# Attention and MLP kernel on one core: loads tied to the first pair, and a new layout of PSUM banks in the first chunk

## The chip, the cores and the metric

One core of a Trainium2 chip. The metric is device time in microseconds (us), the median of several executions. TensorE is called PE below, VectorE DVE, ScalarE ACT, GpSimd POOL, and the queue that issues the loads SP.

## The reference

Two parts, one after the other. The first is a linear attention with a decaying state (batch 4, 8 heads, 768 time steps, head dimension 48):

```
for t in range(S):
    kt, vt, rt = (k[:, :, t], v[:, :, t], r[:, :, t])
    cur = np.einsum('bhd,bhe->bhde', u[None] * kt, vt)
    y[:, :, t] = np.einsum('bhd,bhde->bhe', rt, state + cur)
    state = w[None, :, :, None] * state + np.einsum('bhd,bhe->bhde', kt, vt)
```

The second is an MLP over its 3072 result rows of 384 numbers: `h = x @ w_in` (384 to 2048), exact GELU, then `@ w_out` (2048 to 384). All in float32.

## The kernel before

**Work.** Time is cut into 6 chunks of 128 steps. In a chunk the 8 heads are 4 pairs, and a pair in a chunk is a *group*: 24 groups, numbered by `gi`. A group's operands are `T` (r and k, lanes by time), `N` (k and v, time by lanes). DVE scales `T` by powers of the decay (L357), POOL scales `N` (L363). PE makes `scores` and `own` (L390, keys against queries, into banks `g.x`), `gains` (L401, what the group adds to the state, into columns from `U0` of `g.y`), `old` (L409, the carried state against the queries) and `new` (L419, masked scores against v), both into `g.y`. DVE selects the masked scores into `Am` (L447, `select`). ACT and DVE split the result in `g.y` into a high and a low part (L461, L462, `keep`), which are x of the MLP. ACT or DVE update the state from `gains` (L439, L442, `state`). In the first chunk the 16 rows of padding of a pair's x come from the pair `p = 3`, which is group 0: a matmul `gaps` (L429) brings them from group 0's result `x3`, so the `gaps` of groups 1 to 3 need group 0's `keep`.

**MLP.** 96 *steps* (6 chunks by 16 blocks of 128 hidden units). Step m has nine products into bank `Hp` (L544, `moe1`), GELU twice on ACT (L572, L573), a subtraction on DVE (L574), and nine products into three banks `O` (L585, `moe2`), mostly one step later. Each weight block comes as 64-bit words (`raw`, 768 KB, L301) and in chunk 0 is split into a high and a low float by three ACT and four DVE instructions (L314 to L326, `w_split`). The three `raw` buffers are used in turn.

**Order.** Nothing is ordered by hand. `Plan` collects all operations with a planned length, a due time and the names that they read and write; `run` then puts them into the engines' queues, earliest due first among those whose planned inputs are ready. Semaphores are set by the layer below from the tiles that the instructions really touch; a name given to `Plan` alone orders the queues and makes no semaphore. `GROUP_DUE` says how late in a period of four steps a group is due, `GROUP_AHEAD` how far ahead of that its loads are.

**First chunk.** Groups 0 to 3 (`first_group`) use two sets of PSUM banks in turn (`SETS`): `A` and `Y` for even groups, `AE` and `YE` for odd ones. A bank holding a set's results must be read before the next group of the same set writes it. PE begins with `HEATS` products of zeros, and `plan.filler` may put more of them into planned pauses. Loads are listed by `LOADS`: groups 1 to 5, three weight blocks, and u. Every load also waits for the load eight places ahead of it in the queue, since eight semaphores (`DMAHW0` to `DMAHW7`) are used in turn.

## Time and profile before

| what | value |
|---|---|
| median of 3 executions | 517.97 us (517.8 to 518.02) |
| the profiled execution's own time | 519.95 us |
| its span, first to last instruction | 517.9 us |
| PE, matmuls | 488.1 us, 94% |
| DVE | 245.5 us, 47% |
| ACT | 207.1 us, 40% |
| POOL | 65.7 us, 13% |
| mean granted clock of PE | 0.96 of 2.4 GHz |
| DMA | 43.85 MB, 85 GB/s |

The shares are means over three stages: the first chunk's groups (0 to 41 us), the stage in which weights are still split (to about 135 us), and the rest. A busy PE is not a PE at its peak: matmuls are pipelined, and the granted clock says at which of its two levels (1.2 or 2.4 GHz) it ran.

### The profile page before, as it was taken

The numbers are of one execution on the slowest core, as the hardware profiler recorded it, in microseconds if no ns is written. First come the engines' busy times: TensorE is split into PE (matmuls) and PEld (weight loads), VectorE is DVE, ScalarE is ACT, GpSimd is POOL, SyncE is SP. The second block draws the span as 40 slices with busy tenths as digits, with TensorE's granted clock in tenths as the row PEclk, the third lists the DMA queues.
The fourth block names the chain that finished last, engine by engine and source line by source line (L and its number), as shares of the span: only waits on it lengthen the run. The fifth ranks groups of instructions, "written<-read, shape, count | busy, mean of one in ns | idle before, by whom it ended". The sixth has DMA issues, their size and how long they took to land.

```text
span 517.9 us, 11402 instructions
## 1 busy us (share of the span) xinstructions
PE 488.1 (94%) x5006; PEld 389.5 (75%) x5006; DVE 245.5 (47%) x366; ACT 207.1 (40%) x435; POOL 65.7 (13%) x66
## 2 busy tenths in 40 slices
...
GB/s 224 321 113 63 196 155 221 208 129 92 53 93 92 43 51 92 84 61 94 47 48 92 68 77 92 66 28 92 90 54 92 6 7 10 63 0 1 0 1 65
DMA packets 13190, 43.85 MB, mean 85 GB/s; under 512 B 1808, under 2 KB 2192, under 8 KB 13136
## 3 DMA queue, kind: packets, MB, share of 16 engines
q1 hardware_dynamic: 13136, 43.07, 26.9%
q8 instruction: 41, 0.67, 0.6%
q14 instruction: 13, 0.11, 0.1%
...
## 4 chain that ended last, share of the span: by engine, by line
PE 85%; DVE 6%; issue 3%; DMA 3%; ACT 1%; POOL 1%; SPq 0%; POOLq 0%
PE Hp L544 37%; PE O L585 35%; PE Y L419 3%; PE A L390 3%; PE Y L409 3%; PE Y L401 1%; DMA Nb<-in_rkv_dram 1%; DMA T<-in_rkT_dram 1%; DVE wl L326 1%; PE Y L585 1%; DVE wa L322 1%; DVE Sa L442 1%; PE AE L390 1%; ACT gh L572 1%; DVE gl L574 1%
## 5 line engine op out<-in xcount | busy, mean ns | idle before, releaser
L544 PE MATMUL Hp<-xx,wh 128*128 128x512 f32 x576 | 170.0, 402 | 2.1 <-issue 0.7
L574 DVE TENSOR_TENSOR gl<-gf,gh 128x512 fp32r<-128x512 f32 x95 | 75.9, 799 | 183.4 <-ACT gf L573 183.2
L572 ACT ACTIVATE gh<-Hp 128x512 fp32r<-128x512 f32 x95 | 56.8, 598 | 179.3 <-PE Hp L544 179.1
L544 PEld LDWEIGHTS Hp<-xx,wh 128*128 128x128 f32 x576 | 106.4, 190 | 27.3 <-ACT gf L573 1.8
L544 PE MATMUL Hp<-xx,wl 128*128 128x512 f32 x288 | 84.8, 402 | 1.4 <-DVE wl L326 1.2
L585 PE MATMUL O<-gh,wh 128*128 128x512 f32 (+1 forms) x285 | 81.8, 394 | 2.9 <-ACT gh L572 2.7
L585 PE MATMUL O<-gh,wl 128*128 128x512 f32 (+1 forms) x285 | 80.6, 390 | 0.0
L585 PE MATMUL O<-gl,wh 128*128 128x512 f32 (+1 forms) x285 | 80.6, 390 | 0.0
L585 PEld LDWEIGHTS O<-gh,wh 128*128 128x128 f32 x285 | 52.6, 188 | 19.6 <-ACT gh L572 7.8
L544 PEld LDWEIGHTS Hp<-xx,wl 128*128 128x128 f32 x288 | 54.0, 190 | 17.1 <-DVE wl L326 3.5
L585 PEld LDWEIGHTS O<-gl,wh 128*128 128x128 f32 x285 | 52.6, 188 | 11.8 <-DVE gl L574 0.2
L585 PEld LDWEIGHTS O<-gh,wl 128*128 128x128 f32 x285 | 52.6, 188 | 11.6
L573 ACT ACTIVATE gf<-Hp 128x512 f32<-128x512 f32 x96 | 56.9, 593 | 0.0
L361 POOL TENSOR_TENSOR Nb<-Nb 128x384 f32<-128x384 f32 x16 | 21.0, 1315 | 262.5 <-DMA Nb<-in_rkv_dram 227.2
L381 ACT ACTIVATE Am<-diag,cs 128x64 f32<-128x64 f32 x128 | 33.9, 342 | 27.6 <-DVE cs L376 27.6
L442 DVE SCALAR_TENSOR_TENSOR Sb<-Sa,E,Y 48x192 f32<-48x192 f32 x40 | 16.5, 413 | 35.4 <-ACT xx L461 28.0
L363 POOL TENSOR_TENSOR Nb<-Nb,WN 128x384 f32<-128x384 f32 x20 | 21.5, 1076 | 59.3 <-DMA Nb<-in_rkv_dram 58.1
L461 ACT CAST xx<-Y 112x512 fp32r<-112x512 f32 (+1 forms) x16 | 9.4, 586 | 42.5 <-PE Y L401 38.7
L357 DVE TENSOR_TENSOR Tb<-Tb,E 112x1024 f32<-112x1024 f32 x20 | 24.4, 1219 | 2.3 <-DMA Tb<-in_rkT_dram 2.3
L447 DVE COPY_PREDICATED Am<-past,A 128x512 f32<-128x512 uint32 x22 | 16.2, 736 | 8.9 <-PE A L390 6.0
L373 POOL TENSOR_TENSOR Nb<-Nb,u_sb 128x384 f32<-128x384 f32 x16 | 17.7, 1106 | 0.1
L326 DVE TENSOR_TENSOR wl<-wa,wh 128x768 fp32r<-128x768 f32 x16 | 17.4, 1089 | 0.2
...
## 6 DMA issues: line engine op xcount, KB each, us to landing
...
```

The lines of the kernel that those rows point to most:

```text
L326: add("dve", sdve(n), LATER, lambda: nc.vector.tensor_tensor(out=both(wl), in0=af, in1=both(wh).bitcast(F32), op=ALU.subtract), r=[A_, f"w ...
L357: add("dve", sdve(1024), LATER, lambda: nc.vector.tensor_tensor(out=flat, in0=flat, in1=E[:, 0, g.p].rearrange("l h i -> l (h i)").unsquee ...
L361: add("pool", pool(DM), LATER, lambda: nc.gpsimd.tensor_tensor(out=g.n[:, 0], in0=g.n[:, 0], in1=g.n[:, 1], op=ALU.mult), r=[g.K], w=[g.R])
L363: add("pool", pool(DM), LATER, lambda: nc.gpsimd.tensor_tensor(out=g.kn, in0=g.kn, in1=WN[:, g.p].rearrange("s j d -> s (j d)").unsqueeze( ...
L381: add("act", sact(HALF) + 60, LATER, lambda x=x, b=b: nc.scalar.activation(out=g.am[:, x, b, :], in_=diag2, func=AF.Copy, scale=g.sums[:, ...
L390: nc.tensor.matmul(g.x[times(h), x, col + b * HALF:col + (b + 1) * HALF], lhsT=k_, rhs=g.t[quarter(x), 0, b, times(h)], start=True, stop=True)
L442: add("dve", 420, at, lambda l=l, x=x, more=more: nc.vector.scalar_tensor_tensor(out=g.s[h + 1][quarter(1 - x)], in0=g.s[h][l], scalar=E[l ...
L544: nc.tensor.matmul(O[3], lhsT=wt[j][:, 0, k_ * 128:(k_ + 1) * 128], rhs=x[:, a, k_, :], start=start and k_ == ks[0], stop=stop and k_ == k ...
L572: add("act", 480, LATER, lambda: nc.scalar.activation(out=high, in_=O[3], func=AF.Gelu), r=["H"], w=[GH])
L573: add("act", 480, LATER, lambda: nc.scalar.activation(out=gf, in_=O[3], func=AF.Gelu), r=["H"], w=["gf"])
L574: add("dve", dve(512), LATER, lambda: nc.vector.tensor_tensor(out=low, in0=gf, in1=high.bitcast(F32), op=ALU.subtract), r=["gf", GH], w=[GL])
L585: nc.tensor.matmul(bank(dst)[:, a:b], lhsT=wt[j][:, 1, d * 128:(d + 1) * 128], rhs=gt[:, a:b], start=(j == 0 and n == 0), stop=(j == NJ - ...
```

## The change

The four loads named in `GATED` (weight block 2, groups 4 and 5, u) are given to the planner as readers of `x3h`, the high part of group 0's result, and `w2` goes ahead of group 5 in `LOADS`. Groups 1 to 3 are loaded and planned in the order of their numbers. In the first chunk scores alternate between `AA` and `AE` as before, all four groups share `YU` for `old`, `new` and `gaps`, and `gains` have a tile of their own, `UE`, with a half for even and a half for odd groups. `GROUP_DUE` grows from 9500 to 20000 ns. The hold on the filler is set at the first `gains` and not taken back.

```
-WEIGHT_AHEAD, GROUP_AHEAD, GROUP_DUE = 12500, 28000, 9500
+WEIGHT_AHEAD, GROUP_AHEAD, GROUP_DUE = 12500, 28000, 20000
...
-LOADS = (1, "w0", 2, 3, "w1", 4, 5, "w2", "u")
+LOADS = (1, "w0", 2, 3, "w1", 4, "w2", 5, "u")
+GATED = ("w2", 4, 5, "u")
...
-        AE, YE = (pso.tile([128, 2, 512], F32, name=n) for n in ("AE", "YE"))
+        AE = pso.tile([128, 2, 512], F32, name="AE")
+        UE = pso.tile([128, 2, 512], F32, name="UE")
...
-                (g.x, g.X), (g.y, g.Y) = SETS[i if gi < NP else 0]
+                g.x, g.X = (AE, ["O0", "O1"]) if gi < NP and i else (AA, ["A0", "A1"])
+                g.y, g.Y = YU, ["Y0", "Y1"]
+                g.u, g.U, g.u0 = (UE, ["O2", "H"], i * 256) if gi < NP else (YU, g.Y, U0)
...
-            add("pe", 500, LATER, first_gains, r=[g.K, g.V], w=g.Y)
+            add("pe", 500, LATER, lambda: (setattr(plan, "hold", True), gains(g)), r=[g.K, g.V], w=g.U)
...
+        for gi in range(NP):
+            if gi:
+                load_group(gi, gi + 3)
+            first_group(gi)
...
         for n, x in enumerate(LOADS):
+            early_ = ["x3h"] if x in GATED else []
+            if x in range(NP):
+                continue
...
-                w_load(int(x[1]), n + 3)
+                w_load(int(x[1]), n + 3, early_)
             else:
-                load_group(x, n + 3)
-        for gi in range(NP):
-            first_group(gi)
+                load_group(x, n + 3, early_)
```

How it moves instructions, first on SP: the loads from group 3's (or 2's) first to u. `T_102` to `T_105` and `N_110` to `N_113` are groups 0 to 3, `Tb_106`, `Nb_114` group 4, `Tb_107`, `Nb_115` group 5, `raw_130` weight block 2; in brackets what a load waits for. Before:

```order
L205 DMA T_105<-in_rkT_dram 112x1024
L207 DMA N_113<-in_rkv_dram 128x768
L205 DMA T_104<-in_rkT_dram 112x1024
L207 DMA N_112<-in_rkv_dram 128x768 [waits DMAHW0_49]
L301 DMA raw_128<-in_wmlp_dram 128x1536 [waits DMAHW1_49]
L301 DMA raw_129<-in_wmlp_dram 128x1536 [waits DMAHW2_49]
L205 DMA Tb_106<-in_rkT_dram 112x1024 [waits DMAHW3_49]
L209 DMA Nb_114<-in_rkv_dram 128x768 [waits DMAHW4_49]
L205 DMA Tb_107<-in_rkT_dram 112x1024 [waits DMAHW5_49]
L209 DMA Nb_115<-in_rkv_dram 128x768 [waits DMAHW6_49]
L301 DMA raw_130<-in_wmlp_dram 128x1536 [waits DMAHW7_49]
L696 DMA u_sb<-in_uN_dram 64x384 [waits DMAHW0_49]
```

Now:

```order
L206 DMA T_104<-in_rkT_dram 112x1024
L208 DMA N_112<-in_rkv_dram 128x768
L206 DMA T_105<-in_rkT_dram 112x1024
L208 DMA N_113<-in_rkv_dram 128x768 [waits DMAHW0_49]
L302 DMA raw_128<-in_wmlp_dram 128x1536 [waits DMAHW1_49]
L302 DMA raw_129<-in_wmlp_dram 128x1536 [waits DMAHW2_49]
L206 DMA Tb_106<-in_rkT_dram 112x1024 [waits DMAHW3_49]
L210 DMA Nb_114<-in_rkv_dram 128x768 [waits DMAHW4_49]
L302 DMA raw_130<-in_wmlp_dram 128x1536 [waits DMAHW5_49]
L206 DMA Tb_107<-in_rkT_dram 112x1024 [waits DMAHW6_49]
L210 DMA Nb_115<-in_rkv_dram 128x768 [waits DMAHW7_49]
L700 DMA u_sb<-in_uN_dram 64x384 [waits DMAHW0_49]
```

Groups 2 and 3 have changed places, and weight block 2 has gone ahead of group 5. No load waits for ACT, the engine that writes `x3h`; each waits for one of the eight DMA semaphores alone, as before.

Second on PE: the first chunk, from group 1's `own` to group 1's `new` (a plain matmul of this list is two in the trace, so x16 here is x32 there; the `gaps` are single). Before:

```order
L390 MATMUL AE<-T_103,KB_109 64x64 x16
L401 MATMUL YE<-N_111 48x48 x16
L409 MATMUL Y<-T_102,Sb 48x64 x8
L419 MATMUL Y<-Am_116,N_110 48x64 x16
L390 MATMUL AE<-T_105 64x64 x16
L390 MATMUL AE<-T_105,KB_109 64x64 x16
L390 MATMUL A<-T_104 64x64 x16
L429 MATMUL YE<-x_122,spread 128x256 x4
L409 MATMUL YE<-T_103,Sb 48x64 x8
L419 MATMUL YE<-Am_117,N_111 48x64 x16
```

Now, on to group 3's `own`:

```order
L393 MATMUL AE<-T_103,KB_109 64x64 x16
L412 MATMUL Y<-T_102,Sb 48x64 x8
L422 MATMUL Y<-Am_116,N_110 48x64 x16
L404 MATMUL UE<-N_111 48x48 x16
L393 MATMUL A<-T_104 64x64 x16
L393 MATMUL A<-T_104,KB_108 64x64 x16
L432 MATMUL Y<-x_122,spread 128x256 x4
L412 MATMUL Y<-T_103,Sb 48x64 x8
L422 MATMUL Y<-Am_117,N_111 48x64 x16
L404 MATMUL UE<-N_112 48x48 x16
L393 MATMUL AE<-T_105 64x64 x16
L393 MATMUL AE<-T_105,KB_109 64x64 x16
```

Group 0's `old` and `new` now stand ahead of group 1's `gains`, and one group ends before the next but one begins. Behind this piece come, now, for group 2 `gaps`, `old`, `new`, then group 3's `gains`, `gaps`, `old`, `new`, and the first step of the MLP.

Third on DVE: the first steps of the MLP, around weight block 1 (`wl1_84` is its last piece). Before:

```order
L318 TENSOR_SCALAR wa1_132<-wa1_132 128x768
L357 TENSOR_TENSOR Tb1_107<-Tb1_107,E_98 112x1024
L320 SCALAR_TENSOR_TENSOR wa1_132<-raw1_129,wa1_132 128x768
L447 COPY_PREDICATED Am0_116<-diag2_94,A_67 128x512
L322 ISA wa1_132<-wa1_132,wb1_135 128x1536
L442 SCALAR_TENSOR_TENSOR Sb_97<-Sa_96,E_98,Y_68 48x192 x2
L447 COPY_PREDICATED Am0_116<-past2_95,A_67 128x512
L442 SCALAR_TENSOR_TENSOR Sa_96<-Sb_97,E_98,Y_68 48x192 x2
L326 TENSOR_TENSOR wl1_84<-wa1_132,wh1_76 128x768
L574 TENSOR_TENSOR gl0_125<-gf_127,gh0_123 128x512
```

Now:

```order
L321 SCALAR_TENSOR_TENSOR wa1_132<-raw1_129,wa1_132 128x768
L319 TENSOR_SCALAR wa2_133<-wa2_133 128x768
L323 ISA wa1_132<-wa1_132,wb1_135 128x1536
L569 TENSOR_TENSOR gl0_125<-gf_127,gh0_123 128x512
L321 SCALAR_TENSOR_TENSOR wa2_133<-raw2_130,wa2_133 128x768
L327 TENSOR_TENSOR wl1_84<-wa1_132,wh1_76 128x768
L323 ISA wa2_133<-wa2_133,wb0_134 128x1536
L360 TENSOR_TENSOR Tb1_107<-Tb1_107,E_98 112x1024
L450 COPY_PREDICATED Am0_116<-diag2_94,A_67 128x512
L327 TENSOR_TENSOR wl2_85<-wa2_133,wh2_77 128x768
```

The seven instructions of groups 4 and 5 that stood ahead of `wl1` in the first piece now stand behind it. The same shift by part of a period runs through the rest of the lists. Ahead of step 16 (the second chunk of the MLP), though, both PE lists hold the products of the same groups: `gains` of five and `old` and `new` of four behind the first chunk. Ahead of weight block 15's last DVE instruction the old DVE list has 154 rows and the new one 155: a sum over a group (L376) and a GELU subtraction (L574) more, a state update (L442) less.

## Rows read from the trace of the kernel before

**Rows 1.** Windows: us, busy time (and instructions) of PE, PEld, DVE, ACT, POOL, clock, DMA

```profile
13.00:26.00 13.00, 6.36 (x206) 5.76 (x200) 7.06 (x11) 5.95 (x12) 2.52 (x3) 0.50 1.03 324
39.00:52.00 13.00, 11.15 (x184) 7.88 (x184) 10.91 (x18) 8.53 (x14) 0.00 (x0) 0.70 0.19 63
60.00:135.00 75.00, 69.55 (x697) 51.62 (x696) 69.79 (x96) 48.07 (x75) 9.73 (x7) 1.00 0.45 149
135.00:515.00 380.00, 374.35 (x3416) 302.22 (x3414) 137.18 (x206) 133.08 (x312) 46.83 (x42) 1.00 0.19 57
```

**Rows 2.** Timeline, PE, first chunk: start, duration, engine, line, operation, count, idle before

```profile
18.03 0.45 PE L409 MATMUL Y<-T,Sb 48*48 48x64 f32 x3 [2.76 <-issue]
...
21.14 1.06 PE L390 MATMUL A<-T 48*64 48x64 f32 x27
26.85 0.48 PE L390 MATMUL A<-T 48*64 48x64 f32 x5 [4.65 <-issue]
...
33.74 0.87 PE L401 MATMUL YE<-N 64*48 64x48 f32 x26 [0.32 <-issue]
```

**Rows 3.** The page's table of DMA queues: packets, MB, share of 16 engines

```profile
q8 instruction: 41, 0.67, 0.6%
```

**Rows 4.** Timeline, group 5's operands on POOL and DVE

```profile
28.17 0.99 POOL L363 TENSOR_TENSOR Nb<-Nb,WN 128x384 f32<-128x384 f32 x1 [1.70 <-DMA Nb<-in_rkv_dram]
...
44.16 1.22 DVE L357 TENSOR_TENSOR Tb<-Tb,E 112x1024 f32<-112x1024 f32 x1
```

**Rows 5.** Timeline, PE, ACT and DVE in the first chunk, pieces of one group

```profile
27.26 1.22 PE L429 MATMUL YE<-x,spread 112*128 112x256 f32 x4
28.41 1.09 PE L409 MATMUL YE<-T,Sb 48*48 48x64 f32 x16
29.60 1.10 PE L419 MATMUL YE<-Am,N 64*48 64x64 f32 x32
30.48 1.08 PE L390 MATMUL A<-T,KB 48*64 48x64 f32 x32
31.33 0.86 PE L401 MATMUL Y<-N 64*48 64x48 f32 x32
...
38.90 0.58 ACT L461 CAST xx<-YE 128x512 fp32r<-128x512 f32 x1 [3.56 <-PE YE L419]
...
39.52 0.69 DVE L462 TENSOR_TENSOR xx<-YE,xx 128x512 fp32r<-128x512 f32 x1 [2.14 <-ACT xx L461]
...
39.77 1.11 PE L419 MATMUL Y<-Am,N 64*48 64x64 f32 x32
...
41.21 0.77 PE L544 MATMUL Hp<-xx,wh 128*128 128x512 f32 x1 [0.33 <-DVE Sa L442]
```

**Rows 6.** Timeline, DVE while weights are split, and POOL beside it

```profile
47.51 0.73 DVE L447 COPY_PREDICATED Am<-diag,A 128x512 f32<-128x512 uint32 x1 [1.26 <-PE A L390]
...
60.90 0.55 DVE L318 TENSOR_SCALAR wa<-wa 128x768 int32<-128x768 int32 x1
...
61.37 0.94 DVE L326 TENSOR_TENSOR wl<-wa,wh 128x768 fp32r<-128x768 f32 x1
...
103.53 1.77 DVE L326 TENSOR_TENSOR wl<-wa,wh 128x768 fp32r<-128x768 f32 x1
...
104.56 1.61 POOL L363 TENSOR_TENSOR Nb<-Nb,WN 128x384 f32<-128x384 f32 x1
105.22 1.36 DVE L318 TENSOR_SCALAR wa<-wa 128x768 int32<-128x768 int32 x1
...
106.51 1.75 DVE L326 TENSOR_TENSOR wl<-wa,wh 128x768 fp32r<-128x768 f32 x1
...
128.84 1.52 DVE L326 TENSOR_TENSOR wl<-wa,wh 128x768 fp32r<-128x768 f32 x1
```

**Rows 7.** Chain that ended last: start us, us, what

```profile
42.11 3.78 PE Hp L544 x8
...
156.19 2.10 PE O L585 x9
```

More of the change, by code (lines that the diff above doesn't have):

```diff
@@ L200, in rwkv_gelu_mlp, with load_group @@
         slot = lambda gi: gi if gi < NP else NP + gi % 2
-        def load_group(gi, at):
+        def load_group(gi, at, r=()):
             s = slot(gi)
-            dma(LP * 4096, at, lambda: nc.sync.dma_start(T[s], rkT[gi]), w=[f"T{s}"])
+            dma(LP * 4096, at, lambda: nc.sync.dma_start(T[s], rkT[gi]), r=r, w=[f"T{s}"])
             if gi < NP:
-                dma(C * 3072, at + 1, lambda: nc.sync.dma_start(N[s], rkv[gi, :, 1:]), w=[f"Nk{s}", f"Nv{s}"])
+                dma(C * 3072, at + 1, lambda: nc.sync.dma_start(N[s], rkv[gi, :, 1:]), r=r, w=[f"Nk{s}", f"Nv{s}"])
             elif gi < DIRECT:
-                dma(C * 3072, at + 1, lambda: nc.sync.dma_start(N[s][:, 1:], rkv[gi, :, 1:]), w=[f"Nk{s}", f"Nv{s}"])
+                dma(C * 3072, at + 1, lambda: nc.sync.dma_start(N[s][:, 1:], rkv[gi, :, 1:]), r=r, w=[f"Nk{s}", f"Nv{s}"])
             else:
-                dma(C * 4608, at + 1, lambda: nc.sync.dma_start(N[s], rkv[gi]), w=[f"Nr{s}", f"Nk{s}", f"Nv{s}"])
+                dma(C * 4608, at + 1, lambda: nc.sync.dma_start(N[s], rkv[gi]), r=r, w=[f"Nr{s}", f"Nk{s}", f"Nv{s}"])
         dma(5000, 0, lambda: nc.sync.dma_start(wu_sb, wuT), w=["w_sb"])
@@ L252, in warm_up @@
             for n in range(HEATS):
-                heat((A + [YU[:, 0], YU[:, 1]] + [AE[:, 0], AE[:, 1], YE[:, 0]])[n % 7])
-            plan.filler = lambda: heat(YE[:, 1]), "H", HEAT_NS, HEAT_ROOM
-        add("pe", 430 * HEATS, 10, warm_up, r=["zeros"], w=["H", "A0", "A1", "O0", "O1", "O2", "Y0", "Y1"])
+                heat((A + [YU[:, 0], YU[:, 1]] + [AE[:, 0], AE[:, 1]])[n % 6])
+            plan.filler = lambda: heat(UE[:, 1]), "H", HEAT_NS, HEAT_ROOM
+        add("pe", 430 * HEATS, 10, warm_up, r=["zeros"], w=["H", "A0", "A1", "O0", "O1", "Y0", "Y1"])
         E0, E1 = (E[:, a].rearrange("l p h i -> l (p h) i") for a in range(2))
@@ L298, in rwkv_gelu_mlp, with w_load @@
         wbits = wmlp.bitcast(I32)
-        def w_load(j, at):
+        def w_load(j, at, r=()):
             dma(128 * 6144, at, lambda: nc.sync.dma_start(raw[j % 3].rearrange("p h n t -> p (h n t)"), wbits[:, j]),
-                w=[f"raw{j % 3}"])
+                r=r, w=[f"raw{j % 3}"])
         def w_split(j):
@@ L400, in gains @@
                     for h in range(2 if g.more else 1):
-                        nc.tensor.matmul(g.y[quarter(x), h, U0 + b * D:U0 + (b + 1) * D], lhsT=g.kn[times(h), b, heads(x)],
+                        nc.tensor.matmul(g.u[quarter(x), h, g.u0 + b * D:g.u0 + (b + 1) * D], lhsT=g.kn[times(h), b, heads(x)],
                                          rhs=g.vn[times(h), b, heads(x)], start=True, stop=True)
@@ L436, in state @@
                 l = quarter(x)
-                more = g.y[l, h, U0:U0 + NB * D].rearrange("d (b e) -> d b e", e=D)
+                more = g.u[l, h, g.u0:g.u0 + NB * D].rearrange("d (b e) -> d b e", e=D)
                 if g.c == 0 and h == 0:
                     add("act", 320, at, lambda x=x, more=more: nc.scalar.copy(out=g.s[1][quarter(1 - x)], in_=more),
-                        r=[g.Y[0]], w=[g.S[1][1 - x]])
+                        r=[g.U[0]], w=[g.S[1][1 - x]])
                 else:
@@ L443, in state @@
                         out=g.s[h + 1][quarter(1 - x)], in0=g.s[h][l], scalar=E[l, 1, g.p, h, MID:MID + 1], in1=more,
-                        op0=ALU.mult, op1=ALU.add), r=[g.Y[h], g.S[h][x], "E1"], w=[g.S[h + 1][1 - x]])
+                        op0=ALU.mult, op1=ALU.add), r=[g.U[h], g.S[h][x], "E1"], w=[g.S[h + 1][1 - x]])
         def select(g, mask, MASK, col):
@@ L477, in first_group @@
             add("pe", 600, LATER, lambda: own(g), r=[g.T, f"{g.KB}0", f"{g.KB}1"], w=g.X)
-            def first_gains():
-                gains(g)
-                if gi % 2:
-                    plan.hold = True
-            add("pe", 500, LATER, first_gains, r=[g.K, g.V], w=g.Y)
+            add("pe", 500, LATER, lambda: (setattr(plan, "hold", True), gains(g)), r=[g.K, g.V], w=g.U)
             state(g, 0, LATER)
@@ L492, in first_group @@
             state(g, 1, LATER)
-            if gi % 2:
-                add("do", 0, LATER, lambda: setattr(plan, "hold", False), w=g.Y)
         def products(g, f):
@@ L505, in products @@
                 r += [f.T, f.K, f.V] + ([f"{f.KB}0", f"{f.KB}1"] if f.direct else [])
-                w += f.X + f.Y
+                w += f.X + f.U
                 ns += 1300 if f.direct else 850
```

5 lines of the change are left out of this document (2 added, 3 removed).

## The prediction, made before the changed kernel ran

> **What bounds the kernel now.** I read the windows by stage first. From 135 to 515 us PE is busy for 374.35 of 380 us [rows 1]: there the end moves only by work or idle time of PE itself. From 60 to 135 us PE and DVE are both busy for 93% of the time (69.55 and 69.79 of 75) [rows 1]; 16 weight blocks are split then, and what DVE does later, the MLP does later. In the first chunk it is neither: from 13 to 26 us PE is busy for 6.36 of 13 us, DVE for 7.06, and the DMA engines without a break (share 1.03) [rows 1].
>
> Next the timeline of PE in the first chunk. It stands still three times for nothing that the profile shows: 2.76 us up to 18.03, 4.65 us up to 26.85, and 0.32 us up to 33.74 [rows 2]. Between the first and the second restart lie 126 matmuls (3, three times 32, 27), between the second and the third 127 (5, 4, 16, three times 32, 6). An equal number of instructions each time speaks for the program itself being fetched: the instruction queue moved 41 packets [rows 3] for PE's 10,012 matmuls and weight loads, one per 244. I take it that PE waits for a packet of code, asked for when the packet before is begun, and that it comes late while the data loads fill the DMA engines.
>
> The Trainium skill speaks against this reading (Runtime: NRT & Kernel Launch, Instruction fetch mechanics): the next block is fetched while the current one runs, and crossing into it is "mostly hidden". Here the trace differs with 2.76 and 4.65 us [rows 2], and the sum goes by the trace; by the rule of the Trainium skill these waits would be something else and might stay away, for 511 us instead of 516.7, as the third rival works out from rows.
>
> **The loads.** The change means to hold four loads until group 0's result. In the built queue none waits for ACT; all wait for the same eight DMA semaphores as before. So I cost the holding at nothing, neither gain nor loss. What is left is order. Weight block 2 goes ahead of group 5's two loads, which so come later by 768 KB at 324 GB/s [rows 1], 2.4 us. POOL scales that group at 28.17 now, its T is scaled at 44.16 [rows 4]: some 13 us of cover, without which it would cost those 2.4 us. Groups 2 and 3 swap places with equal sizes: nothing. The zero products stay twelve.
>
> **The first chunk on PE.** I put the new order onto the old restarts. Up to the first stop PE ran 221 matmuls, in the new list 29 of the 32 of group 0's `new` are then through; the second stop falls 8 matmuls into group 1's `new`, the third 4 into group 2's `old`. Up to 26.85 the waits cover all else. From there, with start-to-start times at the same half clock [rows 5]: rest of `new` 0.66 (24 of 32 at 0.88), `gains` 0.86, `scores` and `own` 1.70, `gaps` 1.15, four of `old` 0.2: 31.4. The code that came at 33.74 before [rows 2] comes then again, so PE waits 2.3 instead of 0.32 us. After it: rest of `old` 0.99 (1.19 less 0.2), `new` 0.88, to 35.6. Group 3's `gains` (0.86) hide only part of what follows: all groups now share one tile for results, so group 3's `gaps` wait until group 2's result is read. `new` began at 34.73; 1.17 us after such a beginning ACT reads, 0.62 later DVE starts, 0.69 it takes [rows 5], and 0.1 for the handing over makes 37.3, 0.8 us of idle PE. Then `gaps` 1.15, `old` 1.19, and 1.44 from the beginning of `new` to step 0 (39.77 to 41.21) [rows 5]: 41.1 against 41.21. **Term: -0.1.** Before, PE came to this point late, held by DVE reading the odd set of banks; that wait goes, and the code is late next. If the third packet is there when wanted, step 0 comes 2.3 us sooner; if it needs as long after the second as the second after the first (8.82 us), it lands at 35.67 and step 0 comes 1.8 us later than now. Both ends go into the range.
>
> **The stage of splits.** Ahead of step 16 both PE lists hold the same groups, and DVE's lists to the last weight block are 154 and 155 rows long. The larger `GROUP_DUE` therefore takes no work out of this stage; it changes what stands beside what. Two things follow. First, DVE stood idle for 1.26 us at 47.51, waiting for PE's scores of group 4 [rows 6]; there the new list has pieces of blocks 1 and 2, whose data landed long before. Between nothing and 1.3 us to gain; I take -0.3, near nothing, because DVE has another 0.8 us of idle time between 39 and 52 (10.91 of 13 busy) [rows 1] that such a wait can move into. Second, DVE and POOL get into each other's way. With POOL's three operations of a group beside it, DVE's split pieces took 1.77 and 1.75 instead of 0.94, and 1.36 instead of 0.55 us; a fourth took 1.52 at 128.84 [rows 6]. That is 0.83 + 0.81 + 0.81 + 0.58 = 3.0 us in the stage that DVE bounds. POOL's list is as long in the new program, but falls on other DVE instructions. Bounds: nothing saved, all 3.0 saved, or 0.8 more lost if the fourth place collides fully and a fifth does so. DVE is busy for 93% of this stage, mostly with such pieces, so new collisions are likelier than none: I keep 2.1 of the 3.0, near the row as it is. **Term: -0.9.**
>
> **The clock.** It reads 0.70 over 39 to 52 [rows 1]; at 0.5 first and 1.0 after, it rose 7.8 us in, at 46.8. Step 0 begins at the same time, so I take nothing; rising sooner or later could spare or cost about nine products of 0.47 us at half clock (3.78 for eight) against 0.23 at full clock (2.10 for nine) [rows 7], 2.2 us.
>
> **After 135 us.** Same products, groups behind a step's first half instead of before it. PE has 5.65 us of idle time there [rows 1]; I take no change, and a quarter of it, 1.4, as bound each way.
>
> **Sum.** -0.1 - 0.3 - 0.9 = -1.3 us. The profiled execution took 519.95 us (span 517.9 and 2.05 around it), 1.98 above the median of 517.97; the difference goes onto the median: **516.7 us**. A measurement of this kernel can tell some 0.2% (1.04 us) from no change, so this is a small gain, just beyond that.
>
> **Rivals.** *No change, 517.9.* The collisions come back elsewhere at the same price, the idle 1.26 us too: -0.1 is left. For it: same lists by length, POOL's work unchanged. Against it: three collisions in one group are many. Chance 0.33 for all that ends within 0.2%.
>
> *Slower, 519.5: the third code packet.* The place is group 2's `old`, the price the time that the packet lands after 33.74, one for one, since everything up to step 0 hangs on it. It now meets PE at 31.4, not 33.4, so its lateness is no longer hidden. From 35.0 on it eats the whole -1.3 (33.74 + 1.3); landing at 35.67 it makes +1.8, and with the collisions unimproved 519.7, with a third of their gain 519.5. Against it: the bytes that the data loads move up to then are the same as before. Chance 0.13; with 0.08 more for new waits of PE after 135 us, slower has 0.21.
>
> *Much faster, 511: the waits stay away.* If they are no code packets, or if lighter traffic brings these sooner, then the 2.76 and 4.65 us have no reason to recur. PE would then be held by group data alone; of the 7.4 us some 6 would reach step 0, and DVE with it: 517.97 less 6 is 512, less the 0.9 of the collisions 511. The equal counts speak against it. Chance 0.05. (The Trainium skill, on the page named above, would allow it.) The rest of faster is the forecast (0.30) and its better cases, the third packet in time or the clock up sooner, about 515 (0.11): 0.46 in all.
>
> The range from 514.2 to 519.6 leaves out the much faster case and the worst of the late packet and the late waits, 0.18 together.
>
> **What would show it.** PE's timeline: restarts near 18.0 inside `new` of group 0, near 26.9 inside `new` of group 1, a third one near 33.7 inside `old`, each after 126 or 127 matmuls; an idle 0.8 us ahead of the last `gaps`, waiting for DVE; step 0 at 41.1. On SP no load that waits for ACT. Step 2 some microseconds early, as two split blocks stand ahead of group 5's work on DVE, and step 16, now near 135, about 1.3 us early. In DVE's rows fewer split pieces over 1.3 us. I am wrong if restarts do not follow the count, if step 16 comes later than now, or if PE's idle time after 135 us differs by over 1.4 us.

## The result and the profile after

| | before | changed |
|---|---|---|
| median of the runs (lowest to highest) | 517.88 us (516.64 to 518.02) | 512.63 us (512.32 to 513.59) |
| profiled execution: own time, span | 519.95, 517.9 us | 513.59, 511.9 us |
| PE, DVE busy | 488.1, 245.5 us | 483.7, 240.9 us |
| mean granted clock of PE | 0.96 | 0.97 |

The medians lie 5.25 us apart; the ratio over the runs is 0.9907 (95% interval 0.9887 to 0.9927), which is 4.8 us of 518. The forecast was 1.3 us, and 514.2 was the low end of the range. The windows of the changed kernel, first the stretches of [rows 1], then the first 60 us in three cuts (us, busy time and instructions of PE, PEld, DVE, ACT, POOL, clock, DMA share, GB/s):

```profile
13.00:26.00 13.00, 7.45 (x196) 6.49 (x198) 8.77 (x14) 5.42 (x10) 2.90 (x3) 0.63 1.02 332
39.00:52.00 13.00, 12.31 (x166) 9.66 (x167) 11.62 (x16) 9.65 (x16) 0.00 (x0) 0.90 0.40 125
60.00:135.00 75.00, 67.88 (x780) 51.41 (x782) 66.84 (x92) 46.99 (x80) 10.54 (x8) 1.00 0.46 146
135.00:515.00 380.00, 369.16 (x3323) 298.38 (x3312) 131.17 (x202) 128.71 (x303) 49.32 (x42) 0.99 0.19 57
...
0.00:40.00 40.00, 27.45 (x605) 23.10 (x605) 24.32 (x46) 16.28 (x33) 8.12 (x16) 0.68 0.71 213
40.00:60.00 20.00, 19.20 (x316) 15.23 (x317) 18.53 (x27) 13.41 (x21) 0.00 (x0) 0.96 0.45 141
0.00:60.00 60.00, 46.66 (x920) 38.33 (x921) 42.85 (x73) 29.68 (x54) 8.12 (x16) 0.77 0.62 189
```

The same three cuts of the kernel before:

```profile
0.00:40.00 40.00, 27.03 (x580) 23.08 (x584) 21.00 (x40) 14.32 (x31) 8.12 (x16) 0.62 0.72 213
40.00:60.00 20.00, 17.14 (x324) 12.56 (x320) 17.48 (x27) 11.67 (x19) 1.05 (x1) 0.83 0.42 129
0.00:60.00 60.00, 44.16 (x896) 35.65 (x897) 38.48 (x66) 26.00 (x49) 9.16 (x17) 0.69 0.62 185
```

In the stretch from 135 us PE's smaller busy time is no new idle time: its last product ends at 506.06 instead of 511.42 us. By 40 us PE has done almost the same in both executions (27.03 and 27.45 us busy), DVE 3.3 us more; by 60 us DVE is 4.4 us ahead. From then on the lead stays: step 4 begins at 64.24 instead of 68.77, step 8 at 85.89 instead of 91.31, step 16 at 129.74 instead of 134.77, step 48 at 283.53 instead of 288.82. (Both profiled executions lie above their medians, by 2.1 and 1.0 us, so these leads are somewhat larger than the gain.) PE's timeline of the changed kernel, to be laid beside [rows 2] and [rows 5]:

```profile
17.51 0.34 PE L422 MATMUL Y<-Am,N 64*48 64x64 f32 x2 [1.58 <-issue]
...
22.01 0.33 PE L422 MATMUL Y<-Am,N 64*48 64x64 f32 x8
25.35 0.89 PE L422 MATMUL Y<-Am,N 64*48 64x64 f32 x24 [3.01 <-issue]
...
29.69 0.45 PE L412 MATMUL Y<-T,Sb 48*48 48x64 f32 x3
33.01 0.90 PE L412 MATMUL Y<-T,Sb 48*48 48x64 f32 x13 [2.87 <-issue]
...
36.52 1.22 PE L432 MATMUL Y<-x,spread 112*128 112x256 f32 x4 [0.78 <-DVE xx L465]
...
39.89 0.79 PE L539 MATMUL Hp<-xx,wh 128*128 128x512 f32 x1
```

PE stops as long as before (7.46 us against 7.73 in [rows 2]), 127 matmuls apart. The trace of the changed kernel also records the packets of the instruction queue: at 14.97, 22.81 and 30.44 us, each of 16,384 bytes and 1.1 to 1.3 us long, and PE goes on 1.3 to 1.4 us behind the end of each. In the kernel before they begin at 15.52, 24.07 and 31.28, and PE goes on 1.3 to 1.5 us behind their ends. So these stops are waits for code. What differs between the kernels is what comes right behind a restart. DVE of the kernel before, then of the changed one:

```profile
22.55 0.96 DVE L320 SCALAR_TENSOR_TENSOR wa<-raw,wa 128x768 int32<-128x768 int32 x1
30.77 0.41 DVE L442 SCALAR_TENSOR_TENSOR Sa<-Sb,E,YE 48x192 f32<-48x192 f32 x1 [7.26 <-PE YE L419]
```

```profile
22.55 0.95 DVE L321 SCALAR_TENSOR_TENSOR wa<-raw,wa 128x768 int32<-128x768 int32 x1
26.92 0.69 DVE L465 TENSOR_TENSOR xx<-Y,xx 128x512 fp32r<-128x512 f32 x1 [3.42 <-ACT xx L464]
...
48.50 0.72 DVE L450 COPY_PREDICATED Am<-diag,A 128x512 f32<-128x512 uint32 x1
```

Both stand idle from 23.5. Before, PE came back at 26.85 with group 2's scores, and DVE got a result only at 30.77, 3.9 us later. Now the stop falls inside group 1's `new`, and DVE goes on 1.6 us after the restart. The idle 1.26 us of [rows 6] are gone too in this execution (last row).

### The profile page after: what moved, and what is told of

It is laid out like the page before. It is cut to its first block, busy times and chain, and to the rows that moved or that the text cites. A ratio compares the mean times of both kernels' runs of the same rounds, so it can differ in the third digit from the quotient of the medians.

```text
span 511.9 us, 11420 instructions
## 1 busy us (share of the span) xinstructions
PE 483.7 (94%) x5006; PEld 388.1 (76%) x5006; DVE 240.9 (47%) x366; ACT 205.4 (40%) x435; POOL 68.0 (13%) x66
## 4 chain that ended last, share of the span: by engine, by line
PE 84%; DMA 7%; DVE 3%; issue 3%; ACT 2%; SPq 1%; ACTq 0%
PE Hp L539 37%; PE O L580 36%; DMA raw<-in_wmlp_dram 5%; PE Y L422 3%; PE Y L412 3%; PE A L393 2%; DMA T<-in_rkT_dram 2%; PE Y L404 1%; PE Y L580 1%; DVE Am L450 1%; ACT wa L315 1%; ACT gh L567 1%; PE Y L432 0%; DVE wa L321 0%; PE AE L393 0%
## 5 line engine op out<-in xcount | busy, mean ns | idle before, releaser
L539 PE MATMUL Hp<-xx,wh 128*128 128x512 f32 x576 | 167.1, 398 | 0.0
L569 DVE TENSOR_TENSOR gl<-gf,gh 128x512 fp32r<-128x512 f32 x95 | 71.5, 753 | 187.7 <-ACT gf L568 187.5
L580 PE MATMUL O<-gh,wh 128*128 128x512 f32 (+1 forms) x285 | 83.2, 399 | 6.7 <-ACT gh L567 6.6
L364 POOL TENSOR_TENSOR Nb<-Nb 128x384 f32<-128x384 f32 x16 | 18.1, 1130 | 256.1 <-DMA Nb<-in_rkv_dram 194.4
L366 POOL TENSOR_TENSOR Nb<-Nb,WN 128x384 f32<-128x384 f32 x20 | 27.5, 1377 | 65.1 <-DMA Nb<-in_rkv_dram 63.9
L360 DVE TENSOR_TENSOR Tb<-Tb,E 112x1024 f32<-112x1024 f32 x20 | 25.6, 1282 | 5.5 <-DMA Tb<-in_rkT_dram 4.8
L464 ACT CAST xx<-Y 112x512 fp32r<-112x512 f32 (+1 forms) x18 | 10.6, 586 | 31.0 <-PE Y L404 18.5
L379 DVE TENSOR_REDUCE cs<-Nb 128x8 f32<-128x384 f32 x16 | 8.8, 551 | 28.5 <-POOL Nb L376 28.5
L315 ACT ACTIVATE wa<-raw 128x768 f32<-128x768 f32 x16 | 14.6, 912 | 8.7 <-DMA raw<-in_wmlp_dram 4.3
L465 DVE TENSOR_TENSOR xx<-Y,xx 112x512 fp32r<-112x512 f32 (+1 forms) x18 | 12.4, 692 | 11.4 <-ACT xx L464 11.1
```

What stands on the lines that cost most here:

```text
L315: add("act", sact(n), LATER, lambda: nc.scalar.activation(out=af, in_=hi.bitcast(F32), func=AF.Abs, scale=2.0 ** -112), r=[R_], w=[A_])
L360: add("dve", sdve(1024), LATER, lambda: nc.vector.tensor_tensor(out=flat, in0=flat, in1=E[:, 0, g.p].rearrange("l h i -> l (h i)").unsquee ...
L364: add("pool", pool(DM), LATER, lambda: nc.gpsimd.tensor_tensor(out=g.n[:, 0], in0=g.n[:, 0], in1=g.n[:, 1], op=ALU.mult), r=[g.K], w=[g.R])
L366: add("pool", pool(DM), LATER, lambda: nc.gpsimd.tensor_tensor(out=g.kn, in0=g.kn, in1=WN[:, g.p].rearrange("s j d -> s (j d)").unsqueeze( ...
L539: nc.tensor.matmul(O[3], lhsT=wt[j][:, 0, k_ * 128:(k_ + 1) * 128], rhs=x[:, a, k_, :], start=start and k_ == ks[0], stop=stop and k_ == k ...
L569: add("dve", dve(512), LATER, lambda: nc.vector.tensor_tensor(out=low, in0=gf, in1=high.bitcast(F32), op=ALU.subtract), r=["gf", GH], w=[GL])
```

## The experiments

In microseconds below, a ratio is multiplied by 518. In its three measurements the changed kernel stood at 0.9907, 0.991 and 0.9907.

**The parts of the change.** Theory B: the gain comes from the banks, by a sooner step 0 and clock. Theory D: from the due date. Theory L: from the order of the loads.

`due_only`:
```
-WEIGHT_AHEAD, GROUP_AHEAD, GROUP_DUE = 12500, 28000, 9500
+WEIGHT_AHEAD, GROUP_AHEAD, GROUP_DUE = 12500, 28000, 20000
```


> The kernel before with GROUP_DUE = 20000 alone. Theory B (banks: the 5.3 us come from the first chunk, by the new order of banks, through code that is wanted sooner and a clock that rises sooner): step 0 stays at 41.2, the clock rises near 46.4 as before, 517.0 to 518.0 us. Theory D (due date: split pieces ahead of group 5's work keep DVE and PE busy from step 0 to step 4): step 0 at 41.2, step 4 near 66.5 or sooner in place of 68.77, 514.5 to 516.0 us.

`banks_only`: the kernel before with the change's lines on `AE`, `UE`, `g.x`, `g.y`, `g.u` and the hold, and nothing else.

> The kernel before with the new banks and the filler held from the first group on, loads and GROUP_DUE as before. Theory B: step 0 near 39.9 in place of 41.2, clock up at 41 to 43, 513 to 515 us. Theory D: step 0 near 39.9, the rest as before, 516.5 us. Theory L (order of loads: other traffic brings PE's code sooner, at 17.5, 25.4 and 33.0 in place of 18.0, 26.9 and 33.7): restarts as in the kernel before, step 0 at 41 or later, 517 to 518 us.

`loads_only`: the kernel before with `LOADS`, `GATED`, `early_` and the loop over the first groups.

> The kernel before with the new order of the loads and of the first groups alone; old banks, old GROUP_DUE. Theories B and D: nothing but the noise, 517.3 to 518.3 us, code restarts near 18.0, 26.9, 33.7. Theory L: code restarts near 17.5, 25.4, 33.0 and step 0 some 0.7 to 1.3 us sooner, 515.5 to 517.0 us.

`due_back`: the changed kernel, `GROUP_DUE` 9500.

> The changed kernel with GROUP_DUE back at 9500. Theory B: 512.6 to 514.0 us, step 0 near 39.9. Theory D: the part of the gain between step 0 and step 4 is lost, 515 to 516.5 us, step 0 near 39.9 all the same.

Measured (with a second measurement of two of them, beside the changed kernel on one chip, below):

| kernel | ratio | 95% interval |
|---|---|---|
| due_only | 0.9967 | 0.9945 to 0.9989 |
| due_only_2 | 0.9978 | 0.9956 to 1.0000 |
| banks_only | 0.9938 | 0.9913 to 0.9963 |
| loads_only | 0.9981 | 0.9956 to 1.0006 |
| due_back | 0.9941 | 0.9905 to 0.9977 |
| due_back_2 | 0.9937 | 0.9914 to 0.9960 |
| after_third | 0.9907 | 0.9875 to 0.9939 |

> The changed kernel, unchanged, as the measure for the next two on the same chip: ratio 0.988 to 0.993 to the kernel before.

> The changed kernel with GROUP_DUE back at 9500, once more beside the changed kernel. If the due date is worth what the first two single edits say (1 to 2 us): ratio 0.993 to 0.996, 1 to 2.5 us above the changed kernel. If it is worth nothing: 0.989 to 0.992.

> The kernel before with GROUP_DUE = 20000 alone, once more. If the due date is worth 1 to 2 us by itself: ratio 0.995 to 0.998. If the first measurement was chance: 0.999 to 1.001.

So the banks give 3.2 us (1.9 to 4.5 by the interval), the due date 1.1 to 1.8 (alone or as the last step; 4.8 is the whole), the loads nothing that can be told from none (1.0 us less, by the interval between 2.3 less and 0.3 more). Each single interval is wide; that the due date is worth something rests on the four measurements together. On a kernel of 517.97 us `banks_only` is 514.8 (in Theory B's range), `due_only` 516.3 and 516.8 and `due_back` 514.9 and 514.7 (each between what Theories B and D gave), and `loads_only` 517.0, the end of Theory L's range, with restarts near Theory L's (17.58, 25.84, 33.27). So the gain is shared, most of it by the banks. As for the gate, with `GATED` empty the built lists are the same on all five engines, so that part of the change does nothing.

**Chance and clock.** In one execution the clock rises sooner than in another. 39 to 52 us show 0.90 for the changed kernel, 0.70 before, 0.55 in `due_only`. Theory C: with PE's idle gap ahead of step 0 filled it rises sooner, and that is worth time.

`before_fill`, behind the last `new` of the first chunk:
```
+                if gi == 2:
+                    nc.tensor.matmul(A[0][:, 0:384], lhsT=zeros[:, 0:128], rhs=zeros[:, 0:384], start=True, stop=True)
```
`after_fill`, ahead of group 3's `gaps`:
```
+                        for n in range(2):
+                            nc.tensor.matmul(A[n][:, 0:448], lhsT=zeros[:, 0:128], rhs=zeros[:, 0:448], start=True, stop=True)
```


> The changed kernel once more, unchanged, beside the kernel before on the same chip. If the gain belongs to the program and not to the chance of one execution: ratio 0.988 to 0.994, step 0 at 39.5 to 40.3, DVE idle up to 40 us for 14 to 15 us in place of 17.8, and the clock up within 6 us after PE's last idle stretch, at 41 to 43. If the 5.3 us were mostly chance (the clock's rise falls differently in each execution): ratio 0.995 or more, and the rise anywhere from 41 to 51.

> The kernel before with one zero product of 384 columns behind the last product of group 2, in PE's 0.33 us of idle time ahead of step 0. Theory C (the clock rises only after PE has run on without an idle stretch, and the 0.33 us put the rise off): the rise comes near 42 in place of 46.4 to 46.9, the nine products of step 0 take some 2 us less, DVE's wait of 1.27 us at 47.5 is gone; 1.3 to 2.0 us faster, ratio 0.996 to 0.9975. Rival (0.33 us of idle time do not matter to the clock, or PE's start is late by as much): rise at 46 to 47, ratio 0.999 to 1.001.

> The changed kernel with two zero products of 448 columns in PE's 0.78 us of idle time ahead of the last gaps. Theory C: the rise comes at 37 to 39 in place of 41.5, step 0 and its products sooner, and 0.5 to 1.5 us faster than the changed kernel (DVE, not PE, then sets the pace from step 0 on): ratio 0.986 to 0.990. Rival: the clock as in the changed kernel, ratio as there, 0.990 to 0.992.

Measured: `after_again` 0.9910 (0.9877 to 0.9943), `before_fill` 0.9997 (0.9978 to 1.0015), `after_fill` 0.9909 (0.9889 to 0.9929). Step 0 of `after_again` began at 42.0, outside what was expected, and so were the rise of the clock (43.95) and DVE's idle time up to 40 us (17.75 us; 15.7 in the first execution of the changed kernel, 19.0 in the kernel before): group 1's tile, for which DVE waits, was scaled at 9.56 instead of 8.74 us in that execution. The ratio stayed. The window from 39 to 52 us, of `before_fill`, `after_fill` and `after_third`:

```profile
39.00:52.00 13.00, 11.48 (x247) 8.43 (x251) 12.09 (x20) 8.60 (x14) 0.00 (x0) 0.79 0.21 66
```

```profile
39.00:52.00 13.00, 12.22 (x185) 9.38 (x184) 12.86 (x18) 10.36 (x18) 0.00 (x0) 1.00 0.36 125
```

```profile
39.00:52.00 13.00, 12.77 (x174) 10.10 (x175) 10.50 (x15) 8.17 (x13) 0.00 (x0) 0.70 0.28 95
```

In these single executions the clock rose at 44.55 in `before_fill` (46.86 in the kernel before; it fell again from 54.8 to 58.2) and at 38.79 in `after_fill`, even ahead of step 0, whose step 4 then began at 62.7, sooner than in the changed kernel (64.2); at step 8 nothing was left (86.1 and 85.9). But without any edit the rise moves as far: 41.53, 43.95 and 46.75 in the three profiled executions of the changed kernel. The mean granted clock over whole executions says more. It is 0.967 in the 11 of `before_fill` beside 0.969 in those of the kernel before on that chip, and 0.970 in the 5 of `after_fill` beside 0.969 in those of `after_again`. So that a filled gap brings the rise sooner is not shown, and neither edit gained time.

A price of the clock does show. Over all 255 executions, each compared with the others of its kernel on its chip, 0.01 more of mean clock goes with 1.8 us less time (1.5 to 2.1); this is a correlation. The rise 5.3 us sooner in the first profile is 0.005 of the mean, so about 0.9 us by this estimate. It is not where the gain comes from, though: on the same chip the changed kernel's mean clock was no higher than that of the kernel before (0.969 beside 0.969, 0.965 beside 0.966). With the new banks and the old due date it was 0.967 to 0.969 beside 0.966, at most 0.6 us by this estimate. So the clock has little part in what the banks give.

**What sets PE's stops.** Theory P: packets of PE's code, late because data loads fill the DMA engines. `true_gate` makes the gate real:
```
+        add("act", 120, 6, lambda: nc.scalar.copy(out=T[NP][0:1, 0, 0, 0:1], in_=x3[0:1, 0, 0:1].bitcast(F32)),
+            r=["x3h"], w=["gate"])
         for n, x in enumerate(LOADS):
-            early_ = ["x3h"] if x in GATED else []
+            early_ = ["gate"] if x in GATED else []
```
Its list on SP now has the wait that the changed kernel's had not:
```
L206 DMA Tb_106<-in_rkT_dram 112x1024 [waits DMAHW3_49,Activation_49]
```


> The changed kernel with the gate made real: ACT writes one element of group 4's tile after group 0's result, so that load and all behind it on SP wait for it. Theory P (PE waits for packets of its own code, which are late because the data loads fill the DMA engines): the DMA engines go idle near 17.5 until the gate opens at 19.5 to 20.5, the packet asked for at 17.5 comes within 2 us in place of 5.3, PE's wait of 3.01 us up to 25.35 shrinks to under 1 us; the next packet meets the gated loads. Step 0 at 37.5 to 39, ratio 0.983 to 0.989. Rival F (packets take their 4 to 6 us whatever the loads do, or late data of group 4 take the place of the waits): restarts at 17.5, 25.4, 33.0 or later, ratio 0.990 to 0.996.

In the traces that load is issued at 20.52 instead of 8.74 us.

`late_gate`: the same, with `xx[0]` and `xx00h`, group 1's result. `old_gate`: `loads_only` with the gate of `true_gate`.

> As the kernel with the real gate, but the gate opens after group 1's result in place of group 0's. Theory P: the packet asked for near 23.2 then also finds the DMA engines idle; PE's wait of 3.73 us up to 30.35 shrinks to 1.5 us or less, step 0 at 34 to 36, and DVE, which now waits less, ends its last split piece 1 to 2.5 us sooner than with the first gate: ratio 0.981 to 0.986. Rival: group 4's late data or the late third weight block keep DVE waiting instead, ratio 0.987 to 0.990.

> The kernel before (old banks, old GROUP_DUE) with the new order of loads and the real gate on group 0's result. Theory P: here too the packet asked for while the DMA engines are idle comes within 2 us, but group 0's result comes some 2 us later in this order than with the new banks (20.4 in place of 18.3), so the gate opens near 21.5 and the gain is that of one shorter wait: ratio 0.991 to 0.996. Rival (a real gate only helps with the new banks, as the old order waits for DVE next): ratio 0.998 to 1.001.

`two_gates`: group 4 waits for `x3h`; `w2`, 5 and u for `xx01h`, group 2's result, by a second such copy into `raw[2]`.

> The changed kernel with two real gates: group 4's loads wait for group 0's result, the third weight block, group 5's loads and u for group 2's result. Theory P: the packets asked for near 17.7, 22.6 and 26.1 all find the DMA engines idle or nearly so and come within 2.5 us; none of PE's waits for code after 18 us is longer than 2 us (with the single late gate one is 3.41 us), step 0 at 32 to 34, ratio 0.977 to 0.982. Rival (the third weight block, later by some 3 us, now holds DVE): step 0 at 32 to 34 all the same, ratio 0.982 to 0.986.

Measured: `true_gate` 0.9870 (0.9836 to 0.9903), `late_gate` 0.9818 (0.9785 to 0.9851), `old_gate` 0.9980 (0.9960 to 0.9999), `two_gates` 0.9751 (0.9725 to 0.9777), a median of 506.75 us beside 519.37 and 515.03 for the kernel before and the changed one on that chip: faster than both. The waits for code after 15 us, of `true_gate`, `late_gate` and `two_gates`, all that each has up to 40 us:

```profile
17.83 0.34 PE L422 MATMUL Y<-Am,N 64*48 64x64 f32 x2 [1.52 <-issue]
30.35 0.90 PE L412 MATMUL Y<-T,Sb 48*48 48x64 f32 x13 [3.73 <-issue]
```

```profile
17.68 0.34 PE L422 MATMUL Y<-Am,N 64*48 64x64 f32 x2 [1.50 <-issue]
26.09 0.55 PE L412 MATMUL Y<-T,Sb 48*48 48x64 f32 x13 [0.58 <-issue]
34.31 0.45 PE L422 MATMUL Y<-Am,N 64*48 64x64 f32 x2 [3.42 <-issue]
```

```profile
19.37 0.34 PE L422 MATMUL Y<-Am,N 64*48 64x64 f32 x2 [2.25 <-issue]
```

And the DMA engines around those places, of `true_gate`, then of the changed kernel:

```profile
18.00:22.00 4.00, 4.00 (x109) 3.66 (x109) 3.15 (x7) 3.60 (x8) 0.00 (x0) 0.50 0.33 110
22.00:33.00 11.00, 7.10 (x228) 6.18 (x224) 4.69 (x8) 3.41 (x7) 1.11 (x2) 0.66 1.02 291
```

```profile
18.00:22.00 4.00, 3.92 (x112) 3.53 (x104) 3.31 (x7) 3.84 (x8) 0.18 (x1) 0.62 1.03 307
```

With a DMA share of 0.33 instead of 1.03 behind the first restart, the wait of 3.01 us is gone; the one after it meets the gated loads (share 1.02) and stays. Moving the gate moves the long wait one packet on, and with two gates no wait for code is left behind 19.4. The one up to 19.37 is 2.25 us long, over the 2 us that were expected, and step 0 came at 34.25, a little late; the ratio was better than expected. The packets themselves fit: with the loads held back the next one begins 1.2 to 1.4 us behind PE's first restart (`true_gate`, `late_gate`, `two_gates`), in the kernel before and the changed one 4.4 to 6.0 us behind a restart. Theory P holds at each packet.

How much of the gain of `two_gates` is due to the shorter stops alone is not shown: its mean granted clock is higher too (0.981 beside 0.966 for the kernel before on that chip), which by the estimate above goes with 2.8 us.

`old_gate` missed its expectation. PE's second wait, 4.10 us in `loads_only`, went, but the third grew from 0.87 to 4.22 us, and by the interval the gain is 0 to 2 us. DVE had done no more by step 0 than in the other kernels with the old banks (last table), which fits so small a gain from a step 0 at 38.58; it was not tested.

**What sets the pace from step 0 to step 16.** Theory V: DVE alone. Theory E: PE.

`dve_more` and `pe_more`:
```
+                for _ in range(2 if j in (6, 8, 10, 12) else 1):
+                    nc.vector.tensor_tensor(out=both(wl), in0=af, in1=both(wh).bitcast(F32), op=ALU.subtract)
...
+                        if n == 0 and 6 <= m < 12:
+                            product1(x, j, n, start=True, stop=True)
```


> The changed kernel in which DVE subtracts the low part twice for weight blocks 6, 8, 10 and 12: four pieces of 0.95 us more, 3.8 us, all in the stage of splits. Theory V (from step 0 to the last split piece DVE sets the pace; what counts ahead of it is how long DVE stands idle, not when PE begins step 0): 2.8 to 4.0 us slower than the changed kernel, ratio 0.996 to 1.000 to the kernel before. Rival E (PE sets the pace, the gain came from step 0 and the clock): 0 to 1.5 us slower than the changed kernel, ratio 0.990 to 0.994.

> The changed kernel in which PE does three products of steps 6 to 11 twice: 18 products of 0.21 us more, 3.8 us, in the same stage. Theory V: PE has that much room beside DVE; 0 to 1.5 us slower than the changed kernel, ratio 0.990 to 0.994. Rival E: 3.0 to 4.0 us slower, ratio 0.996 to 1.000.

Measured: `dve_more` 0.9945 (0.9917 to 0.9973), 2.0 us more than the changed kernel for 3.8 us of DVE work; `pe_more` 0.9972 (0.9941 to 1.0003), 3.4 us for 3.8 us of PE work. DVE alone does not seem to set the pace: the interval of `pe_more` lies outside what Theory V gave for it (0.990 to 0.994), if only just. `dve_more` lies between what the two theories gave, and its interval reaches into both, so what DVE's added work costs stays open. The chain of waits of the changed kernel shows a third party, its longest pieces from 55 to 111 us that are no products:

```profile
55.14 6.03 DMA raw<-in_wmlp_dram
...
78.91 8.74 DMA raw<-in_wmlp_dram
...
100.95 10.49 DMA raw<-in_wmlp_dram
```

In the chain of before no weight load stands there. At 78.91 and 100.95 SP issued them right behind a group's two loads. So Theory W: these loads tie both engines.

`weights_first` (and the same edit on `two_gates`, `gates_weights`):
```
-WEIGHT_AHEAD, GROUP_AHEAD, GROUP_DUE = 12500, 28000, 20000
+WEIGHT_AHEAD, GROUP_AHEAD, GROUP_DUE = 40000, 28000, 20000
...
-                out=a, in0=hi, ... r=[R_], w=[A_])
+                out=a, in0=hi, ... r=[R_], w=[A_, f"free{j}"])
...
-                    load_group(gi, at - GROUP_AHEAD)
+                    load_group(gi, at - GROUP_AHEAD, [f"free{G}"] if G < NJ else [])
```


> The changed kernel in which, from group 6 on, a weight block's load stands ahead of a group's two loads in SP's queue instead of behind them. Theory W (in the changed kernel the chain from 55 to 111 us runs for 25 us through three loads of weight blocks, 6.0, 8.7 and 10.5 us long, two of which were issued right behind a group's loads; PE and DVE wait for them in turn, so neither alone sets the pace): these loads leave the chain, 1 to 2.5 us faster than the changed kernel, ratio 0.986 to 0.989. Rival (the waits move: the group's data come later and hold PE and DVE instead): ratio 0.989 to 0.994.

> The kernel with the two real gates, in which from group 6 on a weight block's load stands ahead of a group's loads. Theory W: 1 to 2.5 us faster than with the two gates alone (ratio 0.9751): 0.970 to 0.974. Rival: 0.974 to 0.978.

Measured: `weights_first` 0.9855 (0.9823 to 0.9887), 2.7 us less than the changed kernel; `gates_weights` 0.9756 (0.9726 to 0.9786), as `two_gates`. The share of the chain from 38 to 135 us, of the changed kernel and of `weights_first`:

```profile
by line: DMA raw<-in_wmlp_dram 26.0%; PE O L580 21.1%; PE Hp L539 20.8%; PE Y L422 3.7%; PE Y L412 3.5%; PE A L393 2.9%; issue 2.8%; ACT wa L315 2.8%; ACT gh L567 2.8%; DVE wa L321 2.0%; DVE wl L327 1.8%; ACT wh L325 1.5%; DVE Am L450 1.4%;
```

```profile
by line: PE Hp L539 41.6%; PE O L580 37.3%; PE A L393 5.0%; PE Y L422 4.6%; PE Y L412 4.1%; ACT gh L567 2.5%; PE Y L404 2.5%; issue 2.3%; PE Y L432 0.4%
```

Theory W holds for the changed kernel, though the chain's 26% (25 us) were worth 2.7 us: a share of a chain is no forecast of a gain. With two gates it gave nothing, though there too the chain lost its weight loads. The profiles say where it went: from step 4 to step 16 `gates_weights` took 61.90 instead of 65.21 us, but its step 4 began at 61.18 instead of 57.82. Why it began later was not tested.

**All profiles together** but the two with added work, by the profiled execution's own time, with the start of step 0, DVE's busy time up to there and in the first 60 us, and the time from step 0 to step 4 and from step 4 to step 16:

| kernel | own time | step 0 | DVE by step 0 | DVE by 60 us | steps 0 to 4 | steps 4 to 16 |
|---|---|---|---|---|---|---|
| due_only_2 | 520.13 | 40.53 | 21.31 | 39.05 | 28.42 | 66.61 |
| before | 519.95 | 41.21 | 22.15 | 38.48 | 27.56 | 66.00 |
| loads_only | 519.74 | 40.73 | 22.04 | 38.86 | 28.76 | 66.13 |
| before_fill | 519.34 | 40.52 | 22.23 | 38.60 | 28.21 | 66.36 |
| due_only | 518.93 | 41.02 | 21.51 | 38.64 | 28.03 | 66.34 |
| due_back_2 | 517.93 | 42.14 | 24.32 | 39.85 | 25.66 | 66.26 |
| after_third | 516.09 | 42.51 | 24.39 | 39.34 | 24.73 | 64.58 |
| old_gate | 515.97 | 38.58 | 21.93 | 41.60 | 26.82 | 66.25 |
| due_back | 515.95 | 40.05 | 24.24 | 40.83 | 26.15 | 65.93 |
| after_fill | 515.74 | 40.51 | 23.88 | 43.16 | 22.20 | 67.45 |
| banks_only | 514.97 | 39.84 | 24.44 | 42.67 | 25.17 | 66.25 |
| after_again | 513.98 | 42.01 | 24.26 | 40.60 | 24.19 | 64.21 |
| changed | 513.59 | 39.89 | 24.24 | 42.85 | 24.35 | 65.50 |
| weights_first | 510.37 | 40.45 | 25.66 | 43.90 | 23.74 | 62.33 |
| true_gate | 509.56 | 37.23 | 24.18 | 44.75 | 24.25 | 64.38 |
| two_gates | 507.41 | 34.25 | 22.88 | 47.82 | 23.57 | 65.21 |
| gates_weights | 507.24 | 36.13 | 24.78 | 47.19 | 25.05 | 61.90 |
| late_gate | 506.80 | 34.69 | 25.46 | 48.67 | 22.61 | 65.53 |

The time goes with DVE's work by 60 us, but that is partly the same thing told twice: a kernel that is ahead has also done more by 60 us. The start of step 0 says less (39.9, 42.0 and 42.5 in three executions of the changed kernel, 40.5 to 41.2 in the five kernels with the old banks and no real gate). What does not move from one execution to the next is DVE's work ahead of step 0. In the six profiles with the new banks that have neither a real gate, nor a fill, nor the weights ahead it is 24.2 to 24.4 us, in the six with the old banks 21.3 to 22.2: two state updates and a split piece more are done, and the last piece of the first weight block is through instead of just begun. From step 0 to step 4 these take 24.2 to 26.2 us and 26.8 to 28.8. This is a correlation over kernels; no run changed DVE's order by itself.

## Why the prediction was wrong

- **What bounds the kernel:** right that the first 135 us decide; from step 16 to PE's last product the profiled executions differ by 0.3 us. PE's idle time after 135 us stayed, as taken: of the 5.65 us that the prediction read from the window 3.6 lie behind PE's last product, which leaves 2.1 before and 1.9 now. Two of the sixteen weight blocks are split ahead of 60 us, not behind.
- **The loads:** right. No load waits for ACT, and `loads_only` is within its interval of no change. What a real gate brings, 2.1 us in `true_gate` over the changed kernel on the same chip by the ratios (the two intervals overlap), and 8.1 with two, the change as built does not get.
- **PE's stops:** right in place and count (29 of group 0's `new`, 8 of group 1's, 3 of group 2's `old`; 127 matmuls apart). The assumption that they end at the same times was off by 0.5, 1.5 and 0.7 us, and that is chance: in the other two executions of the changed kernel the restarts came at 19.04, 27.19, 35.12 and 19.54, 27.69, 35.62, later than in the kernel before. In each trace a packet begins only behind the restart before it, so a shift of one is handed on to the next. The Trainium skill (Runtime: NRT & Kernel Launch, Instruction fetch mechanics) calls such crossings "mostly hidden"; the trace disagrees while the loads fill the DMA engines (3.01 and 2.87 us) and agrees where they do not (`two_gates`, none behind 19.4).
- **Step 0, the term of -0.1:** the idle 0.8 us ahead of the last `gaps` came as forecast (0.78 in each of the three executions). Step 0 at 39.89 instead of 41.1 was luck of one execution, with 42.01 and 42.51 in the others; over these and the three of `banks_only` and `due_back` with the same banks the mean is 41.1, as the sum had it.
- **The step that failed** is the sentence "Term: -0.1", which took the start of step 0 as all that the first chunk hands on. The sum had no term for the work that DVE gets done meanwhile: up to step 0 that is 24.24 instead of 22.15 us, 2.1 more, as in all executions of the two layouts (last table). The way from step 0 to step 4 then took 24.35 instead of 27.56 us, and step 2 came at 50.33 instead of 60.10. `banks_only` measures what the new order in the first chunk is worth: 3.2 us where the sum had 0.1 (and step 0 of its profile, at 39.84, gives 1.4 of them at most). That it works through DVE is read from the traces; no run tried it alone.
- **The idle 1.26 us, the term of -0.3:** gone altogether in the first profile; between 40 and 60 us DVE was busy 1.05 us longer. In `after_third`, though, DVE stood idle for 1.72 us at 47.87 and was busy for 17.45 us between 40 and 60, as before. So what became of this term lies between nothing and -1.3 and is not settled.
- **Collisions, the term of -0.9:** right in size. DVE's pieces beside POOL's work in the changed kernel, of which two are split pieces over 1.3 us instead of four:

```profile
63.90 1.40 DVE L569 TENSOR_TENSOR gl<-gf,gh 128x512 fp32r<-128x512 f32 x1
...
86.14 1.51 DVE L569 TENSOR_TENSOR gl<-gf,gh 128x512 fp32r<-128x512 f32 x1
...
111.17 1.53 DVE L327 TENSOR_TENSOR wl<-wa,wh 128x768 fp32r<-128x768 f32 x1
...
112.62 1.36 DVE L319 TENSOR_SCALAR wa<-wa 128x768 int32<-128x768 int32 x1
```

  Against 0.69, 0.94 and 0.55 for such a piece alone that is 0.71 + 0.82 + 0.59 + 0.81 = 2.9 us. Before it was 3.0 for the pieces in [rows 6] and 0.8 for a GELU subtraction of 1.50 us at 130.28 that the prediction did not count, 3.8 in all. In `banks_only`, with the old due date, six such pieces from 60 us on came to 4.6, among them

```profile
76.83 1.78 DVE L322 CUSTOM_DVE_ANT_0 wa<-wa,wb 128x1536 uint16<-128x1536 uint16 x1
...
99.80 1.77 DVE L326 TENSOR_TENSOR wl<-wa,wh 128x768 fp32r<-128x768 f32 x1
```

  so from `banks_only` to the changed kernel 1.7 us of collisions go, the size of the measured 1.6 (the order of the loads is in both). It is so in every kernel without a real gate: DVE's pieces that took over 0.2 us longer beside POOL than alone add up, from 60 to 135 us, to 3.8 to 4.5 us in the six with the old due date and to 2.0 to 2.9 in the nine with the new one. So the due date takes collisions away, whatever the banks; that its 1.1 to 1.8 us come from them fits in size and was not tried by itself.
- **The clock, taken as nothing:** right by the mean of the executions (0.969 beside 0.969 and 0.965 beside 0.966 on the same chips). In the profiled execution it rose some 5 us sooner (0.90 against 0.70); in the other two it rose at 43.95 and 46.75.
- **The rivals:** the third packet was not late (33.01) in the first profile and came at 35.12 and 35.62 in the other two, the place that the rival gave it (35.67), but these two took 513.98 and 516.09 us, not 519.5. The waits did not stay away, and "no change" fell with the ratio. The forecast's sign was right, its size a quarter.
